# RetNet attention and snake layer on one core: a new order of steps for the first blocks, constants made on the chip

## The chip, the cores and the metric

The kernel runs on one core of a Trainium2 chip. The metric is the device time of one execution in microseconds (us), lower is better. Five engines work side by side, each through its own queue in order: TensorE (PE) multiplies, VectorE (DVE), ScalarE (ACT) and GpSimd (POOL) work on elements, SyncE (SP) issues transfers. ACT and POOL can issue transfers as well.

## The reference, cut to what matters

```python
def _attn_ref(q, k, v):              # q, k, v: 8 batches, 8 heads, 576 tokens, 64 wide, float32
    scores = scale * np.matmul(q, k.transpose(0, 1, 3, 2))
    gamma = 1.0 - 2.0 ** (-5.0 - np.arange(H))
    Dmat = np.where(rel >= 0, gamma[:, None, None] ** rel[None, :, :], 0.0)   # rel = i - j
    return np.matmul(scores * Dmat[None], v)

def _moe_ref(x, w_in, w_out, alpha):  # x: the attention's output as 4608 x 512
    h = x @ w_in                      # 512 x 2048
    s = np.sin(alpha * h)
    g = h + s * s / (alpha + 1e-09)
    return g @ w_out                  # 2048 x 512
```

## The kernel before

Eight batches of 576 tokens are cut into two tiles p of 256 tokens each and an end of 64 tokens (a 512 KB load brings one tile of q, k or v); the eight ends together make a ninth block. So there are nine blocks of 512 rows for the snake layer: block n is the first 512 tokens of batch n. A batch has four chunks c of 128 tokens, whose sums of k times v are carried from one to the next with a decay.

The steps, by the names that the code gives them:

- `load` lets SP issue one 512 KB load into one of six buffers; a load waits until the cast of the load six places before it has emptied the buffer. `load_w_in(g)` and `load_w_out(g)` let POOL issue a quarter of a weight matrix, cast to float16 on the way; group g of w_in serves the projections 4g to 4g+3.
- `cast` turns q and k to float16 with their decay factors, v without, on the engine named (V is DVE, A_ is ACT, G_ is POOL); the last argument picks a half of the tile. `turn` transposes a tile on PE with the identity (8 products), `take` copies the result out; `crossed` does both by a transposing transfer of SP instead.
- `scores(p, y, bank)` multiplies k by q (16 products), `masked` applies the mask and copies to float16 on DVE. `outer` makes the chunk sums (32 products a tile); `take_sum`, `evict` and `evict_bank` copy them out, `next_sum` (DVE) and `more` (POOL) carry the sum on, `to_state` scales it to float16. `values(p, same, bank)` multiplies scores by v in two groups, `add_states` adds the carried part, `keep` copies the result to the input x of the block.
- `project(n, u, bank)` multiplies block n by column group u of w_in (four products of 512 columns, or two times four of 256), `sine` (ACT), `square` (named engine) and `product` (DVE) make the snake function, and only the product frees the bank. `gemm2(n, u, bank)` adds a quarter of the second multiplication for row group u // 4 (part u % 4 needs `load_w_out(u % 4)`), `finish` copies out and lets SP store.
- `keep_busy(k, bank, m)` issues k products of m columns on zeros that nothing reads.

PSUM has six places: h0, h1, h2 and op of one bank, m0 and m1 of two. A step that wants a place waits until the last reader of the one before is done.

The order within each engine is the order of a list written out by hand for blocks 0 to 2 (lines 593 to 1073); waits between engines follow from the data and the places. Then a loop over n from 3 to 8 (line 1078) runs 16 units per block, each a projection of block n and a `gemm2` of block n - 1, with batch n + 1's attention between; `relay` names the engine through which PE is told that the first group of values is done. In block 3, batch 4's scores and chunk sums stand at units 0, 4 and 8; in the later blocks the scores stand at units 3 and 8 and the chunk sums were made a block earlier.

The identity (for `turn`) and the mask (for `masked`) are constants in memory that ACT's queue loads at the start, behind the decay factors `cn` and ahead of alpha and a small identity `eye` (for `turn_alpha`).

## Time and profile before

| | |
|---|---|
| median of 3 runs | 312.68 us (312.37 to 313.18) |
| profiled execution | 312.64 us |
| its span, first to last instruction | 310.9 us |
| granted TensorE clock over the span | 0.995 |
| busy: PE, DVE, ACT, POOL | 296.9, 206.9, 182.5, 140.8 us |
| moved by transfers | 49.96 MB |

Busy time of PE contains the drain of its products, so a full row does not yet mean that it runs at its peak. In rows of the order of time the columns are start and duration in us, engine, line, operation, output and inputs, shape and count; in brackets stands the idle time before the row and what ended it. A row can hold several instructions merged. In rows of groups the columns behind the bar are busy us, mean ns of one, and idle us before.

### The profile page before, as it was taken

What the parts mean: (1) busy time and instruction counts of PE and PEld (TensorE: products, weight loads), DVE (VectorE), ACT (ScalarE), POOL (GpSimd) and SP (SyncE); (2) the same over time, 40 slices, a digit from 0 to 9 for tenths busy, and PEclk for the clock granted to TensorE, in tenths of its full rate; (3) what the DMA queues carried; (4) which work ended last, traced back from release to release, by engine and by line L of the source; (5) the groups of instructions that cost most, each with busy time, mean ns of one, the idle gap of its engine ahead of it and who ended that gap; (6) DMA issues with size and microseconds to landing.
All of it is one profiled execution on the core that took longest, in us unless ns stands there. A gap on an engine that the chain in (4) does not pass through costs nothing.

```text
span 310.9 us, 7835 instructions
## 1 busy us (share of the span) xinstructions
PE 296.9 (96%) x3238; PEld 149.8 (48%) x3238; DVE 206.9 (67%) x284; ACT 182.5 (59%) x291; POOL 140.8 (45%) x151
## 2 busy tenths in 40 slices
PE   8669989999999999999999999999999999999995
PEld 3444645445554544454445444544454454444443
DVE  2578998689778798575766676656676745655600
ACT  1327952678457767775677567756764556455411
POOL 2855665984919656988275927470030000000000
PEclk9998999999999999999999999999999999999999
DMA  8999999899897679959799969863431111111133
GB/s 208 289 230 261 227 251 257 211 235 222 215 252 222 103 117 309 235 92 184 176 299 164 244 177 282 108 135 84 105 78 44 34 36 36 34 34 35 39 92 75
DMA packets 103108, 49.96 MB, mean 161 GB/s; under 512 B 44944, under 2 KB 98592, under 8 KB 103072
## 3 DMA queue, kind: packets, MB, share of 16 engines
q1 hardware_dynamic: 98192, 44.99, 65.1%
q0 software_dynamic: 4224, 4.19, 8.0%
q8 instruction: 25, 0.41, 0.6%
q10 hardware_dynamic: 656, 0.28, 0.4%
q14 instruction: 11, 0.09, 0.1%
HBM read 36.85 MB, written 9.44 MB: 149 GB/s over the span
## 4 chain that ended last, share of the span: by engine, by line
PE 83%; DMA 7%; DVE 3%; ACT 3%; issue 2%; POOL 0%; ACTq 0%; DVEq 0%
PE ops L552 38%; PE hps L509 37%; DMA w_in<-in_moe_w_in_dram 3%; PE o L374 3%; PE sc L334 3%; DMA v<-in_v_dram 2%; ACT s_t L517 2%; DMA q<-in_q_dram 1%; PE kv L275 1%; DVE q L162 1%; DVE gT L533 1%; DVE ss_t L528 1%; PE o L396 1%; ACT ss_t L526 1%; POOL v L105 0%
## 5 line engine op out<-in xcount | busy, mean ns | idle before, releaser
L552 PE MATMUL ops<-w_out,gT 128*128 128x512 f16 (+2 forms) x592 | 143.4, 374 | 1.3 <-DMA w_out<-in_moe_w_out_dram 1.2
L517 ACT ACTIVATE s_t<-hps,alpha_t 128x512 f16<-128x512 f32 x144 | 97.7, 685 | 75.0 <-PE hps L509 74.4
L533 DVE SCALAR_TENSOR_TENSOR gT<-ss_t,inva,hps 128x512 f16<-128x512 f16 x144 | 106.0, 745 | 50.9 <-ACT ss_t L526 46.6
L509 PE MATMUL hps<-xT,w_in 128*128 128x512 f16 (+1 forms) x568 | 128.5, 361 | 2.1 <-DVE gT L533 1.2
L509 PEld LDWEIGHTS <-w_in 128*128 128x128 f16 x632 | 61.3, 98 | 66.4 <-issue 3.3
L552 PEld LDWEIGHTS <-gT 128*128 128x128 f16 x592 | 56.0, 98 | 64.2 <-issue 2.0
L528 DVE TENSOR_TENSOR ss_t<-s_t 128x512 f16<-128x512 f16 x67 | 38.6, 576 | 22.0 <-ACT s_t L517 21.5
L526 ACT ACTIVATE ss_t<-s_t 128x512 f16<-128x512 f16 x69 | 43.3, 631 | 1.6 <-DVE gT L533 0.5
L345 DVE TENSOR_TENSOR ret<-sc,mask 128x1024 f16<-128x1024 f32 x32 | 38.8, 1219 | 3.8 <-PE sc L334 3.8
L162 POOL TENSOR_TENSOR k<-k,cn 128x1024 f16<-128x1024 f32 (+1 forms) x17 | 29.4, 1730 | 23.9 <-DMA k<-in_k_dram 23.9
L103 ACT COPY osb<-ops 128x512 f32<-128x512 f32 (+1 forms) x33 | 19.2, 580 | 17.2 <-PE ops L552 13.9
L162 POOL TENSOR_TENSOR q<-q,cn 128x512 f16<-128x512 f32 (+1 forms) x16 | 24.6, 1553 | 7.7 <-DMA q<-in_q_dram 7.7
L317 POOL TENSOR_TENSOR kvs<-s,kvs 128x256 f32<-128x256 f32 x23 | 17.2, 747 | 5.2 <-ACT kvs L103 3.7
L103 ACT CAST xT<-o 128x1024 f16<-128x1024 f32 (+1 forms) x14 | 13.3, 957 | 9.0 <-PE o L396 8.9
L146 POOL TENSOR_TENSOR ks<-ks,cn 128x512 f16<-128x512 f32 x4 | 4.2, 1042 | 28.0 <-PE o L374 25.3
L509 PE MATMUL hps<-xS,w_in 128*128 128x512 f16 x64 | 16.4, 379 | 0.0
L528 POOL TENSOR_TENSOR ss_t<-s_t 128x512 f16<-128x512 f16 x8 | 9.3, 1163 | 14.7 <-ACT s_t L517 14.4
L316 POOL TENSOR_TENSOR s<-kvs,cn 128x256 f32<-128x256 f32 x23 | 14.1, 613 | 3.6 <-ACT kvs L103 3.3
L105 POOL CAST v<-v 128x1024 f16<-128x1024 f32 (+1 forms) x15 | 15.1, 1005 | 0.9 <-DMA v<-in_v_dram 0.8
L309 POOL TENSOR_TENSOR s<-kvs,cn 128x256 f16<-128x256 f32 x19 | 12.1, 639 | 6.2 <-DVE kvs L105 4.2
L103 ACT COPY kvs<-kv 128x256 f32<-128x256 f32 (+2 forms) x15 | 7.9, 548 | 10.1 <-PE kv L275 8.4
L374 PE MATMUL o<-ret,v 64*64 64x128 f16 x512 | 12.1, 220 | 1.5 <-DVE ret L345 0.7
(53 smaller groups left out, 135.1 us busy)
## 6 DMA issues: line engine op xcount, KB each, us to landing
out_dram<-osb SPq DMA_DIRECT2D x70, 128.0 KB, 3.4
q<-in_q_dram SPq DMA_DIRECT2D x16, 512.0 KB, 7.2
k<-in_k_dram SPq DMA_DIRECT2D x16, 512.0 KB, 5.2
v<-in_v_dram SPq DMA_DIRECT2D x16, 512.0 KB, 6.4
w_in<-in_moe_w_in_dram POOLq DMA_DIRECT2D x4, 512.0 KB, 9.6
w_out<-in_moe_w_out_dram POOLq DMA_DIRECT2D x4, 512.0 KB, 9.6
ks<-in_k_dram SPq DMA_DIRECT2D x8, 128.0 KB, 4.7
qs<-in_q_dram SPq DMA_DIRECT2D x8, 128.0 KB, 3.7
```

The costliest lines, as they stand in the source:

```text
L103: eng.copy(d_, s_)
L105: eng.tensor_copy(d_, s_)
L162: eng.tensor_tensor(dst[:, a0:a1].rearrange("p a r t d -> p t (a r) d"), t_.rearrange("p (t a) x -> p t a x", t=2)[:, :, a0:a1].rearrange( ...
L317: nc.gpsimd.tensor_tensor(self.kvs[:, c], s32, self.kvs[:, c], ADD)
L345: nc.vector.tensor_tensor(ret.rearrange("p t (z x) -> p (t z) x", z=2), sc.rearrange("p t (z x) -> p (t z) x", z=2), mask[:, 0:256].unsque ...
L374: made.append(matmul(o[t][halves(e), c : c + 128], v16[halves(g), 4 * t + 2 * x + e, r, :], self.ret[p, x][halves(g), t, m : m + 128], sta ...
L509: matmul(hps_of[n, fc][0][:, cols], w_in16[:, a, fc * P : (fc + 1) * P], xs[n][:, a, cols], start=(a == 0 and part != 1), stop=(a == KT - ...
L517: nc.scalar.activation(s_t, hps, mybir.ActivationFunctionType.Sin, bias=0.0, scale=alpha_t[:, fc : fc + 1],)
L526: nc.scalar.activation(ss_t, s_t, mybir.ActivationFunctionType.Square)
L528: eng.tensor_tensor(ss_t, s_t, s_t, MULT)
L533: nc.vector.scalar_tensor_tensor(gT[n][:, fc, :], ss_t, inva[:, fc : fc + 1], hps, MULT, ADD)
L552: matmul(ops[n, c, cols.start][:, cols], gT[n][:, fk, c * P : (c + 1) * P], w_out16[:, fk, cols], start=(fk == 0), stop=(fk == FC - 1), sk ...
```

## The change

The list for blocks 0 to 2 is replaced. k is loaded and turned ahead of q; 12 idle products of 512 columns stand at the start and 7 of 256 columns after batch 0's last chunk sums, where 24, 4 and 1 of 512 stood before. Batch 0's casts, masks and carried sums go mostly to DVE, batch 1's second tile (`q` and `k` of p = 1) is turned before the first projection, the weight groups are loaded in the order 1, 0, 2, 3, and four projections of block 1 (one of them half done) stand ahead of the first `gemm2` of block 0. Batch 4's chunk sums, which block 3 made before, stand at the end of the list, so that block 3 runs as blocks 4 to 6 do; both relays of blocks 3 to 5 go through POOL, where one went through SP. The identity and the mask are made by POOL with `memset` and `affine_select`; their two loads are gone. `wait_for_w_out` is not called any more.

The diff, with the two lists cut to their beginnings:

```diff
-    tok = 2 * ii + hi
-    mask_np = np.concatenate(
-        [(2 * ii + r)[:, None] <= tok[None, :] for r in range(2)] + [ii[:, None] <= np.arange(64)[None, :]], axis=1
-    ).astype(np.float16)
-
-    ident_dram = nc.inline_tensor(np.eye(P, dtype=np.float16), name="rt_ident")
-    mask_dram = nc.inline_tensor(mask_np, name="rt_mask")
...
+    def make_constants():
+
+        ge = mybir.AluOpType.is_ge
+        nc.gpsimd.memset(ident, 0.0)
+        nc.gpsimd.affine_select(
+            out=ident, in_=ident, compare_op=mybir.AluOpType.not_equal, fill=1.0,
+            base=0, pattern=[[-1, P]], channel_multiplier=1,
+        )
+        nc.gpsimd.memset(mask, 1.0)
+        for g in range(2):
+            m = mask[halves(g), 0:256].rearrange("p (r g i) -> p r g i", r=2, g=2)
+            nc.gpsimd.affine_select(
+                out=m, in_=m, compare_op=ge, fill=0.0,
+                base=0, pattern=[[-1, 2], [1, 2], [2, 64]], channel_multiplier=-2,
+            )
+            m = mask[halves(g), 256:320]
+            nc.gpsimd.affine_select(
+                out=m, in_=m, compare_op=ge, fill=0.0, base=0, pattern=[[1, 64]], channel_multiplier=-1,
+            )
+
     with tc.manual_schedule():
         nc.scalar.dma_start(cn, cn_dram.ap())
-        nc.scalar.dma_start(ident, ident_dram.ap())
-        nc.scalar.dma_start(mask, mask_dram.ap())
+        make_constants()
...
-keep_busy(2, "h0")
-keep_busy(8, "op")
-keep_busy(10, "op")
-keep_busy(4, "op")
-load(0, "q", 0)
-cast(0, "q", 0, G_, (1,))
-cast(0, "q", 0, V, (0,))
-turn(0, "q", 0, "h0")
-load(0, "k", 0)
-cast(0, "k", 0, G_, (0,))
-cast(0, "k", 0, V, (1,))
-turn(0, "k", 0, "op")
-take(0, "q", 0, A_)
-take(0, "k", 0, V, (0,))
-take(0, "k", 0, V, (1,))
-load(0, "k", 1)
-cast(0, "k", 1, G_)
-load(0, "q", 1)
-cast(0, "q", 1, V)
-load_w_in(0)
-turn(0, "k", 1, "h1")
-take(0, "k", 1, A_)
-at[0].scores(0, 1, "m0")
-keep_busy(4, "h2")
-load(0, "v", 0)
-at[0].masked(0, 1)
-turn(0, "q", 1, "h2")
-take(0, "q", 1, V)
-cast(0, "v", 0, G_)
-at[0].outer((0,), "op", "h0")
-load_w_in(1)
-at[0].take_sum(0, A_)
-load(0, "v", 1)
-cast(0, "v", 1, G_)
-at[0].scores(1, 0, "m1")
-at[0].outer((1,), "op", "h1")
-at[0].masked(1, 0)
-at[0].take_sum(1, A_)
-at[0].more(1)
-at[0].scores(0, 0, "m0")
-at[0].masked(0, 0)
-at[0].scores(1, 1, "m1")
-at[0].masked(1, 1)
-keep_busy(1, "h2")
-at[0].values(0, False, "m0")
-turn_alpha()
-at[0].to_state(0, G_)
-at[0].to_state(1, V)
-at[0].take_sum(2, A_)
-at[0].more(2)
-at[0].next_sum(3)
-at[0].to_state(2, G_)
-load_w_in(2)
-load(1, "q", 0)
-at[0].values(0, True)
-at[0].add_states(0)
-at[0].keep(0, A_)
-at[0].values(1, False, "h2", "h0")
-at[0].values(1, True)
-at[0].add_states(1)
-project(0, 0, "m1", 0)
-load(1, "k", 0)
-at[0].keep(1, A_, V)
-project(0, 0, "m1", 1)
-take_alpha()
-sine(0, 0)
-cast(1, "q", 0, V, (1,))
-cast(1, "q", 0, V, (0,))
-square(0, 0, V)
...
+keep_busy(1, "op")
+keep_busy(6, "h0")
+load(0, "k", 0)
+cast(0, "k", 0, V)
+keep_busy(5, "op")
+load(0, "q", 0)
+load(0, "k", 1)
+load(0, "q", 1)
+turn_alpha()
+cast(0, "q", 0, V)
+cast(0, "k", 1, V)
+cast(0, "q", 1, G_, (1,))
+turn(0, "q", 0, "h0")
+turn(0, "k", 0, "h1")
+turn(0, "k", 1, "h2")
+take(0, "k", 0, A_)
+take_alpha()
+take(0, "q", 0, V)
+at[0].scores(0, 1, "m0")
+cast(0, "q", 1, V, (0,))
+take(0, "k", 1, V)
+at[0].scores(0, 0, "m1")
+at[0].masked(0, 0)
+load(0, "v", 0)
+cast(0, "v", 0, A_)
+load_w_in(1)
+turn(0, "q", 1, "op")
+load(0, "v", 1)
+take(0, "q", 1, A_)
+at[0].outer((0,), "h0", "h1")
+at[0].masked(0, 1)
+at[0].scores(1, 1, "m0")
+load_w_in(0)
+at[0].take_sum(0, A_)
+at[0].scores(1, 0, "m1")
+cast(0, "v", 1, V, (0,))
+cast(0, "v", 1, V, (1,))
+at[0].outer((1,), "op", "h2")
+load_w_in(2)
+at[0].to_state(0, G_)
+load(1, "k", 1)
+cast(1, "k", 1, G_)
+keep_busy(7, "h0", 256)
+turn(1, "k", 1, "h0")
+take(1, "k", 1, A_)
+at[0].next_sum(1)
+at[0].next_sum(2)
+at[0].to_state(1, V)
+at[0].masked(1, 1)
+at[0].values(0, False, "m0")
+at[0].masked(1, 0)
+at[0].values(0, True)
+at[0].add_states(0)
+at[0].keep(0, A_)
+at[0].to_state(2, V)
+at[0].values(1, False, "m1")
+at[0].values(1, True)
+at[0].add_states(1)
+load_w_in(3)
+at[0].keep(1, A_)
+load(1, "q", 1)
+cast(1, "q", 1, V, (0,))
+cast(1, "q", 1, G_, (1,))
+turn(1, "q", 1, "h1")
+take(1, "q", 1, A_)
+load(1, "k", 0)
+project(0, 5, "h0", 0)
+project(0, 5, "h0", 1)
+project(0, 4, "op", 0)
+project(0, 4, "op", 1)
+sine(0, 5)
+sine(0, 4)
+square(0, 4, A_)
+project(0, 6, "h2")
+sine(0, 6)
+square(0, 6, G_)
+project(0, 2, "h1")
+at[1].scores(1, 1, "m0")
+sine(0, 2)
+invert_alpha()
+square(0, 2, A_)
+project(0, 0, "h0")
+sine(0, 0)
+project(0, 3, "m1")
+sine(0, 3)
+at[0].next_sum(3)
+at[0].to_state(3, V)
+cast(1, "k", 0, G_)
+square(0, 5, V)
+product(0, 5)
+product(0, 4)
+at[1].masked(1, 1)
+project(0, 9, "m0")
+sine(0, 9)
+product(0, 6)
+product(0, 2)
+square(0, 0, G_)
+square(0, 3, V)
+load_w_out(0)
+square(0, 9, A_)
+project(0, 7, "op", 0)
+project(0, 7, "op", 1)
+sine(0, 7)
+project(0, 1, "h2")
+sine(0, 1)
+product(0, 3)
+load(1, "q", 0)
+product(0, 9)
+cast(1, "q", 0, G_)
+product(0, 0)
+square(0, 7, A_)
+load(1, "v", 0)
+product(0, 7)
+square(0, 1, A_)
+at[1].scores(1, 0, "m1")
+turn(1, "k", 0, "h1")
+take(1, "k", 0, V)
+project(0, 15, "m0")
+product(0, 1)
+sine(0, 15)
+square(0, 15, A_)
+product(0, 15)
+at[1].masked(1, 0)
+cast(1, "v", 0, G_)
+project(0, 8, "op")
+sine(0, 8)
+square(0, 8, G_)
+turn(1, "q", 0, "h0")
+project(0, 13, "h1")
+load(1, "v", 1)
+product(0, 8)
+cast(1, "v", 1, G_)
+take(1, "q", 0, A_)
+sine(0, 13)
+at[1].outer((0,), "h2", "h0")
+at[1].take_sum(1, A_)
+load_w_out(1)
+at[1].take_sum(0, A_)
+at[1].to_state(0, G_)
+at[1].more(1)
+load_w_out(2)
+at[1].scores(0, 1, "m1")
+square(0, 13, A_)
+at[1].scores(0, 0, "m0")
+at[1].masked(0, 0)
+at[1].outer((1,), "op", "h2")
+product(0, 13)
+at[1].take_sum(3, A_)
+at[1].masked(0, 1)
+project(0, 10, "h0")
+project(0, 12, "h2")
+project(0, 11, "h1")
+at[1].to_state(1, G_)
+sine(0, 10)
+at[1].values(1, False, "m0")
+at[1].values(0, False, "m1")
+at[1].values(0, True)
+at[1].add_states(0)
+at[1].next_sum(2)
+at[1].values(1, True)
+at[1].to_state(2, V)
+at[1].keep(0, V)
+at[1].add_states(1)
+square(0, 10, V)
+sine(0, 11)
+product(0, 10)
+sine(0, 12)
+project(0, 14, "op")
+square(0, 11, G_)
+project(1, 0, "m1", 0)
+at[1].keep(1, A_)
+square(0, 12, A_)
+load_w_out(3)
+product(0, 12)
+sine(0, 14)
+square(0, 14, A_)
+project(1, 7, "m0")
+sine(1, 7)
+product(0, 11)
+project(1, 1, "h0")
+product(0, 14)
+square(1, 7, A_)
+product(1, 7)
+load(2, "q", 1)
+project(1, 8, "h2")
+gemm2(0, 0, "h1")
+project(1, 0, "m1", 1)
+project(1, 9, "op")
+sine(1, 8)
+gemm2(0, 1, "h1")
...
+at[4].outer((0, 1), "m1")
...
-        h, m = cycle(("h2", "h0", "h1")), cycle(("m0", "m1"))
+
+        h, m = cycle(("h1", "h2", "h0")), cycle(("m0", "m1"))
-        S_ = nc.sync
-                if n == 3:
-                    at_unit(0, lambda: A.scores(0, 0, next(m)), lambda: A.scores(0, 1, next(m)))
-                    behind(0, lambda: A.masked(0, 0))
-                    behind(1, lambda: A.masked(0, 1))
-                    at_unit(4, lambda: A.outer((0, 1), next(m)), lambda: A.scores(1, 0, next(m)), lambda: A.evict((0, 1)))
-                    behind(4, lambda: A.chain((0, 1, 2, 3)), lambda: A.masked(1, 0))
-                    at_unit(8, lambda: A.scores(1, 1, next(m)))
-                    behind(8, lambda: A.masked(1, 1))
-                else:
-                    at_unit(3, lambda: A.scores(0, 0, next(m)), lambda: A.scores(0, 1, next(m)))
-                    behind(3, lambda: A.masked(0, 0))
-                    behind(4, lambda: A.masked(0, 1))
-                    at_unit(8, lambda: A.scores(1, 0, next(m)), lambda: A.scores(1, 1, next(m)))
-                    behind(8, lambda: A.masked(1, 0))
-                    behind(9, lambda: A.masked(1, 1))
-                at_unit(12, lambda: A.values(0, False, next(m), relay=G_), lambda: A.values(1, False, next(m), relay=S_ if n < 6 else G_))
+                at_unit(3, lambda: A.scores(0, 0, next(m)), lambda: A.scores(0, 1, next(m)))
+                behind(3, lambda: A.masked(0, 0))
+                behind(4, lambda: A.masked(0, 1))
+                at_unit(8, lambda: A.scores(1, 0, next(m)), lambda: A.scores(1, 1, next(m)))
+                behind(8, lambda: A.masked(1, 0))
+                behind(9, lambda: A.masked(1, 1))
+                at_unit(12, lambda: A.values(0, False, next(m), relay=G_), lambda: A.values(1, False, next(m), relay=G_))
```

More of the change, by code (lines that the diff above doesn't have):

```diff
@@ L915 @@
         product(1, 13)
[L916 to L930 removed]
+        finish(0, 2)
         at[2].values(0, True)
@@ new lines @@
+        at[2].to_state(3, V)
+        product(1, 11)
+        gemm2(1, 2, "op")
+        project(2, 5, "h2", 0)
+        project(2, 5, "h2", 1)
+        at[3].outer((0, 1), "m0")
+        at[3].scores(0, 1, "m1")
+        square(2, 1, G_)
+        product(2, 1)
+        at[3].evict((0, 1), A_)
+        sine(2, 5)
+        at[3].masked(0, 1)
+        at[3].more(1)
+        square(2, 5, A_)
+        product(2, 5)
+        load(4, "v", 0)
+        load(4, "v", 1)
+        at[3].more(2)
+        cast(3, "q", 1, G_, (0,))
```

595 lines of the change are left out of this document (230 added, 365 removed).

## The prediction

> **What bounds the kernel now.** I read the page first, for the shares and the clock.
>
> ```profile
> span 310.9 us, 7835 instructions
> PE 296.9 (96%) x3238; PEld 149.8 (48%) x3238; DVE 206.9 (67%) x284; ACT 182.5 (59%) x291; POOL 140.8 (45%) x151
> PE 83%; DMA 7%; DVE 3%; ACT 3%; issue 2%; POOL 0%; ACTq 0%; DVEq 0%
> ```
>
> TensorE (PE) is the bound, and the chain that ended last is mostly its own work. Next came the table of busy time by stretch; each row gives PE, PEld, DVE, ACT and POOL busy, then the granted clock, the DMA share and GB/s.
>
> ```profile
> 15.00:20.00 5.00, 2.30 (x98) 1.68 (x98) 4.68 (x8) 0.37 (x1) 4.76 (x8) 1.00 1.20 220
> 20.00:25.00 5.00, 3.74 (x67) 2.17 (x67) 2.77 (x5) 2.29 (x4) 1.05 (x2) 0.72 1.18 258
> 25.00:30.00 5.00, 5.00 (x27) 2.55 (x26) 4.73 (x9) 3.79 (x6) 2.39 (x4) 0.94 1.17 267
> 35.00:40.00 5.00, 5.00 (x43) 3.55 (x41) 4.56 (x8) 4.62 (x10) 2.82 (x3) 1.00 1.18 235
> 145.00:155.00 10.00, 10.00 (x77) 4.61 (x75) 7.26 (x10) 5.87 (x10) 3.85 (x4) 1.00 0.93 139
> ```
>
> In the loop (last row) PE never pauses. The loss lies at the start: PE is busy for less than half of 15 to 20 us, then runs at a granted clock of 0.72. From 25 us on it is full, but DVE and ACT are nearly full beside it, and the transfer engines are full throughout. So I listed PE's order of time, to find each place where it waits.
>
> ```profile
> 1.22 7.69 PE L565 MATMUL idle<-zero 128*128 128x512 f16 x24 [1.22 <-DVE zero L591]
> 21.77 1.53 PE L509 MATMUL hps<-xT,w_in 128*128 128x256 f16 x8 [0.15 <-ACT xT L103]
> 23.96 9.62 PE L509 MATMUL hps<-xT,w_in 128*128 128x512 f16 x48 [0.66 <-DMA w_in<-in_moe_w_in_dram]
> 33.41 0.61 PE L195 MATMUL tr<-ident,k 128*128 128x128 f16 x8
> 33.86 1.03 PE L509 MATMUL hps<-xT,w_in 128*128 128x512 f16 x4
> 42.39 1.02 PE L552 MATMUL ops<-w_out,gT 128*128 128x512 f16 x4 [1.19 <-DMA w_out<-in_moe_w_out_dram]
> 66.66 1.03 PE L509 MATMUL hps<-xT,w_in 128*128 128x256 f16 x8 [0.69 <-DVE gT L533]
> 109.99 1.89 PE L509 MATMUL hps<-xT,w_in 128*128 128x512 f16 x8 [0.55 <-DVE gT L533]
> 119.39 0.71 PE L275 MATMUL kv<-v,k 64*64 64x64 f16 x64
> ```
>
> The first projection starts at 21.77 us. Behind it PE waits four times: 0.66 (w_in), 1.19 (w_out), 0.69 and 0.55 us (a bank that a product still held). A row contains the drain of its last matmul: the turn at 33.41 shows 0.61, yet the next work starts 0.45 later. So a wait costs about 0.16 more than its idle time, and the four together 3.09 + 4 x 0.16 = 3.7 us.
>
> The profiled execution took 312.64 us: the span of 310.9 and 1.74 around it. The median of the runs is 312.68. I sum against 312.64. The tail and the loop blocks 4 to 7 keep their work; the 64 products of batch 4's chunk sums (0.71 us at 119.39) move from block 3 into the list, at no net cost. What the change is worth is therefore the change in PE's lost time before block 3.
>
> **Part 1: the way to the first projection.** The new list hands nearly all of batch 0 to DVE, so I add up DVE's program order. It needs the landings and these durations:
>
> ```profile
> 5.08 0.69 DVE L162 TENSOR_TENSOR q<-q,cn 128x512 f16<-128x512 f32 x1 [3.91 <-DMA q<-in_q_dram]
> 7.16 0.69 DVE L162 TENSOR_TENSOR k<-k,cn 128x512 f16<-128x512 f32 x1 [1.39 <-DMA k<-in_k_dram]
> 9.05 1.90 POOL L162 TENSOR_TENSOR k<-k,cn 128x1024 f16<-128x1024 f32 x1 [0.30 <-DMA k<-in_k_dram]
> 10.82 1.22 DVE L162 TENSOR_TENSOR q<-q,cn 128x1024 f16<-128x1024 f32 x1 [0.22 <-DMA q<-in_q_dram]
> 12.68 1.03 POOL L105 CAST v<-v 128x1024 f16<-128x1024 f32 x1 [0.85 <-DMA v<-in_v_dram]
> 13.65 0.69 DVE L105 COPY qT<-tr 128x1024 f16<-128x1024 f16 x1 [0.39 <-PE tr L195]
> 12.03 1.23 DVE L345 TENSOR_TENSOR ret<-sc,mask 128x1024 f16<-128x1024 f32 x1
> 18.56 0.56 DVE L309 TENSOR_TENSOR s<-kvs,cn 128x256 f16<-128x256 f32 x1
> 19.05 0.84 DVE L304 SCALAR_TENSOR_TENSOR kvs<-kvs,cn,kv 128x64 f32<-128x64 f32 x4
> 48.16 0.46 DVE L105 CAST v<-v 128x512 f16<-128x512 f32 x1
> 20.46 0.93 PE L374 MATMUL o<-ret,v 64*64 64x128 f16 x32
> 5.12 1.55 POOL L162 TENSOR_TENSOR q<-q,cn 128x512 f16<-128x512 f32 x1 [4.67 <-DMA q<-in_q_dram]
> ```
>
> The six loads of batch 0 land 1.85 us apart (5.0, 7.1, 9.0, 10.8, 12.65, so 14.5), whichever tile is first. DVE: cast of k0 5.1 + 1.22 = 6.3; of q0 7.15 + 1.22 = 8.4; of k1 10.25; take of q0 and half a cast of q1 to 11.6; take of k1 to 12.3; two masks to 14.8; the two halves of v1 to 15.7; two next_sums to 17.4; to_state to 17.95; two masks to 20.4; to_state(2) to 20.95; half a cast of the new q(1,1) to 21.65. PE's steps stand inside these times. Behind the last mask PE has two groups of values (0.93 by its row, drain included) and the states, and then the turn of q(1,1), 0.45 behind its cast. The first projection starts at about 22.2, 0.4 later than now. But two turns of batch 1 (2 x 0.45) are done by then that came later before: net -0.5. The 12 idle products, at 0.32 each on the mean of the 24 in the first row and 0.43 at half speed (twice 0.86 / 4, below), end by 6.4, in a gap; the 7 short ones lie in the wait for k(1,1)'s cast on POOL, about 16 to 18: 0. Cover gone, each would cost its 0.1 us.
>
> POOL makes identity and masks with two memsets and five selections, which the trace does not show. The nearest rows:
>
> ```profile
> 0.24 0.10 POOL L1184 MEMSET const-float32-0.0<- 128x1 f32 x1 [0.24 <-issue]
> 29.56 1.03 POOL L528 TENSOR_TENSOR ss_t<-s_t 128x512 f16<-128x512 f16 x1 [2.61 <-ACT s_t L517]
> ```
>
> Seven at 0.10 to 1.03 us are 0.7 to 7.2 us, ended by 7.6. The identity, made first, is wanted at 8.4, POOL's half cast at 10.8. I take 0. Two small transfers fewer ahead of the loads can only gain a little, down to -0.3.
>
> **Part 2: the clock.** Five us at 0.72 and five at 0.94 withhold 5 x 0.28 + 5 x 0.06 = 1.7 us; about 0.5 of it fell into the wait for w_in, where it cost nothing. PE is again sparse from 6 to 22, so I expect one such stretch again, now under continuous projections: +0.5. The ends are -1.2 (no slow stretch) and +2.2 (two).
> The Trainium skill, "TensorE: Matmul & The Clock Gate", section "Why this matters for your kernels", warns of idle gaps beyond about 3 us and gives back the full clock after about 3.4 us of work. This speaks against taking 17 idle products out. The trace agrees in so far as the slow stretch followed the sparse one.
>
> **Part 3: waits that go.** Projections (0,5), (0,4), (0,6) now use w_in's group 1, loaded first; the first multiplication by w_out comes after 19 projections, not 15, so both DMA waits go. The two waits for DVE (0.69, 0.55) belong to the old order. All four: -3.7. What is late next is part 4.
>
> **Part 4: waits that come.** Block 0's elementwise work is squeezed in with batch 1's masks.
>
> ```profile
> L517 ACT ACTIVATE s_t<-hps,alpha_t 128x512 f16<-128x512 f32 x144 | 97.7, 685 | 75.0 <-PE hps L509 74.4
> L526 ACT ACTIVATE ss_t<-s_t 128x512 f16<-128x512 f16 x69 | 43.3, 631 | 1.6 <-DVE gT L533 0.5
> L533 DVE SCALAR_TENSOR_TENSOR gT<-ss_t,inva,hps 128x512 f16<-128x512 f16 x144 | 106.0, 745 | 50.9 <-ACT ss_t L526 46.6
> 40.57 1.00 ACT L103 COPY qT<-tr 128x1024 f16<-128x1024 f16 x1
> 16.07 0.37 ACT L103 COPY kvs<-kv 128x256 f32<-128x256 f32 x1 [1.17 <-PE kv L275]
> 26.54 0.42 DVE L528 TENSOR_TENSOR ss_t<-s_t 128x512 f16<-128x512 f16 x1
> 14.39 0.42 PE L334 MATMUL sc<-qT,kT 64*64 64x128 f16 x16 [0.19 <-DVE qT L105]
> ```
>
> PE from 22.2: two projections at half speed (2 x 1.72), eight at 0.86, the 1.03 of a row less its drain (6, 2, 0, 3, 9, 7, 1, 15), two score groups (0.35 each behind one another) and a turn reach 33.7. Projection (0,8) then needs the bank that product (0,7) frees. DVE has queued from about 28.1 one mask, one square (0.4) and six products (4.5), and product 7 also waits for ACT's square: ready near 34.8. Wait 1.0. Then (0,8), a turn and (0,13) reach 37.0, where outer wants the bank that ACT's take of q(1,0) empties. ACT has from 24.0 eleven sines (7.5), six squares (3.8) and the take (1.0), 36.3 without a gap, 37.4 with the gaps at its start: wait 0 to 0.8, I take 0.7. A chunk sum on ACT holds the next bank 0.4 more. Together 2.1. With the ordering so tight the bounds are 0 and 4.5, which doubles each wait. DVE's queue from 29.3 to the end of block 0 (fourteen products 10.4, three masks 3.7, two squares, a take, a sum, a state and a keep 4.1) is 18.2 us, done at 47.5 to 49; PE's, with these waits, near 50. So nothing more piles up.
>
> From 50 to 110 us I found cushions of 1 to 4 us at the steps of batches 2 and 3. Banks wanted 0.1 to 0.2 us early occur a few times: I take 0.5, bounds 0 and 2. Loop: both relays now sit in POOL's queue; the second stands right behind the first, the casts after both: 0.
>
> **Sum:** -0.5 + 0.5 - 3.7 + 2.1 + 0.5 = -1.1; 312.64 - 1.1 = 311.5, against the median 312.68 a gain of 0.4%.
>
> **The rivals.**
>
> *The late tile (slower).* The first projection now stands behind q(1,1), the eighth load, and POOL's w_in transfers share the engines.
>
> ```profile
> 10.89 0.93 POOL L93 DMA_DIRECT2D w_in<-in_moe_w_in_dram  x1
> 24.30 1.14 POOL L162 TENSOR_TENSOR k<-k,cn 128x512 f16<-128x512 f32 x1 [3.95 <-DMA k<-in_k_dram]
> ```
>
> The eighth load landed at 24.3 where 1.85 spacing gives 18.2, because w_in, issued at 10.89, crowded it from about 16.3 on: 8 us for a load of 1.85, 4.3 times slower. The first w_in is now issued behind POOL's half cast (1.14 to 1.55 from 10.8), at 12 to 12.4, some 1.2 to 1.5 us later; the load then lacks 0.35 to 0.65 of its 1.85 when the crowding begins and lands at 19.2 to 20.5. It decides from 20.95 on: each us later costs one. Landing at 24.3 as now, half a cast on POOL (1.1) and the turn put the first projection at 26: +3.8, 315.3. For it: the margin is only 0.5 to 1.7 us. Against: the later issue.
>
> *The elementwise engines (slower).* If part 4 meets its upper bounds, +2.4 and +1.5: up to 315.4; half of it gives 313.5 to 314. For it: 4.56 and 4.62 of 5 us busy at 35 to 40.
>
> *Two slow stretches (same).* The stretch lost 1.7 us of clock in this execution; a second one under continuous projections is +1.7: 313.2. For it: PE stays sparse longer, without its fillers; against: projections leave no gap from 22.2 on. The Trainium skill's same page, section "What's actually happening", has windows that run free of the kernel's start, so that a boundary can fall badly; no row here shows two in a row.
>
> *No new waits (faster).* Part 4 at nothing: -3.7, 308.9.
>
> **How the numbers follow.** A measurement of this kernel tells 0.3%, 0.94 us, from no change. Forecast 0.42; late tile 0.17; elementwise engines 0.18; two stretches 0.10; no new waits 0.13. Faster: 0.13 and four fifths of the forecast, 0.46. Slower: both slow cases and a little of the third, 0.37. The rest, 0.17, within. The forecast's own range is 310.5 to 312.5; the range over the cases is 308.8 to 315.5.
>
> **What would show it.** Right: first projection near 22.2, no wait of PE on w_in or w_out, one stretch below full clock between 20 and 30, waits of about 2 us on ACT and DVE between 33 and 40, block 3 starting a little sooner for the work done. Wrong: a PE wait for q(1,1)'s cast or turn, POOL busy with the constants beyond 8 us, or waits behind 50 us that sum to over 2.

## The result, and the profile after

The changed kernel is slower: 314.64 us median (20 runs, 312.91 to 317.72) against 312.61 (20 runs of the kernel before, 312.03 to 314.59), a ratio of 1.0056 with an interval of 1.0034 to 1.0078. Here and below, a ratio leaves out the executions in the slower state (317.72 here), so it need not be the quotient of the medians. The forecast was 311.5, a gain; the median lies inside the range over all cases, on the other side of no change, and outside the forecast's own 310.5 to 312.5. The executions of the changed kernel fall into two groups, nine of the 20 at 312.9 to 313.3 us and eleven at 314.3 to 317.7, so a profile of each is read here: one of 313.06 us (span 311.3) and, from a second set of runs of the same kernel, one of 317.0 (span 315.3). The clock averaged over the span doesn't tell the groups apart (0.976 to 0.989 in the short executions, 0.975 to 0.995 in the long ones), so one profile of the long group can't say what each of its executions pays.

The page of the 313.06 us profile, the shares and the chain that ended last:

```profile
span 311.3 us, 7778 instructions
PE 297.3 (95%) x3212; PEld 150.7 (48%) x3212; DVE 211.3 (68%) x297; ACT 184.4 (59%) x291; POOL 132.4 (43%) x143
PE 75%; DMA 10%; DVE 7%; SPq 2%; ACT 2%; POOL 1%; issue 1%; DVEq 0%; ACTq 0%; POOLq 0%
```

Work moved from POOL (140.8 to 132.4) to DVE (206.9 to 211.3), and DVE's share of the chain rose from 3% to 7%. PE's order of time in the same profile shows where that is; the brackets give PE's idle time and what ended it:

```profile
22.48 0.88 PE L189 MATMUL tr<-ident,q 128*128 128x128 f16 x8
23.20 3.66 PE L503 MATMUL hps<-xT,w_in 128*128 128x256 f16 x24
...
38.17 0.45 PE L269 MATMUL kv<-v,k 64*64 64x64 f16 x32 [0.26 <-POOL v L99]
...
43.62 0.31 PE L390 MATMUL o<-qT,s 64*64 64x128 f16 x8 [0.78 <-DVE s L303]
...
60.63 0.71 PE L269 MATMUL kv<-v,k 64*64 64x64 f16 x64 [0.16 <-DVE gT L527]
...
96.74 0.42 PE L328 MATMUL sc<-qT,kT 64*64 64x128 f16 x16 [1.29 <-DVE gT L527]
...
108.55 2.75 PE L503 MATMUL hps<-xT,w_in 128*128 128x512 f16 x12
112.88 1.02 PE L546 MATMUL ops<-w_out,gT 128*128 128x512 f16 x4 [1.58 <-DVE gT L527]
```

The first projection starts at 23.20. The waits for w_in and w_out are gone. Two long new waits, 1.29 and 1.58 us, both for a place that DVE's product frees, lie at 96.74 and 112.88. The second of them is in the loop: of the three projections in the row at 108.55, the third, from 110.28 on, is the first of block 3. The same view of the 317.0 us profile:

```profile
21.62 0.62 PE L189 MATMUL tr<-ident,q 128*128 128x128 f16 x8
22.08 2.19 PE L503 MATMUL hps<-xT,w_in 128*128 128x256 f16 x16
...
40.32 0.45 PE L269 MATMUL kv<-v,k 64*64 64x64 f16 x32 [2.44 <-POOL v L99]
...
64.53 0.70 PE L269 MATMUL kv<-v,k 64*64 64x64 f16 x64 [1.59 <-DVE gT L527]
...
100.65 0.42 PE L328 MATMUL sc<-qT,kT 64*64 64x128 f16 x16 [1.28 <-DVE gT L527]
...
116.79 1.02 PE L546 MATMUL ops<-w_out,gT 128*128 128x512 f16 x4 [1.58 <-DVE gT L527]
```

Here the first projection starts 1.1 us **earlier**, yet the execution ends 3.9 later: outer((1,)) of batch 1 waits 2.44 in place of 0.26, outer of batch 2 waits 1.59 in place of 0.16. The two late waits of the other profile are in this one too, with the same length. PE also waits twice for w_in, 0.35 at 25.48 and 0.40 at 29.10. What differs ahead of 22 us is the clock (columns as before: PE, PEld, DVE, ACT, POOL busy, granted clock, DMA share, GB/s), first in the 313.06 us profile, then in the 317.0 one:

```profile
5.00:10.00 5.00, 2.62 (x21) 1.33 (x19) 3.72 (x4) 0.68 (x1) 0.00 (x0) 0.94 1.17 290
10.00:15.00 5.00, 4.06 (x96) 3.42 (x100) 4.66 (x7) 2.63 (x5) 4.14 (x5) 0.50 1.17 290
15.00:20.00 5.00, 4.57 (x91) 3.20 (x79) 5.00 (x12) 0.96 (x1) 4.04 (x4) 0.50 1.20 243
20.00:25.00 5.00, 4.82 (x100) 4.19 (x98) 2.83 (x10) 3.46 (x5) 0.00 (x0) 0.69 1.20 218
```

```profile
5.00:10.00 5.00, 2.60 (x21) 1.86 (x18) 3.69 (x4) 0.00 (x0) 0.00 (x0) 0.80 1.17 289
10.00:15.00 5.00, 3.33 (x115) 2.68 (x115) 4.74 (x7) 3.32 (x5) 4.12 (x5) 0.85 1.17 290
15.00:20.00 5.00, 2.62 (x83) 1.89 (x75) 5.00 (x12) 1.01 (x1) 4.00 (x4) 1.00 1.20 243
20.00:25.00 5.00, 4.73 (x100) 3.37 (x100) 3.47 (x12) 4.16 (x5) 0.00 (x0) 1.00 1.19 216
```

In the faster execution the clock is at half from 9.4 to 23.06 us, in the slower one only from 8.05 to 11.46. So the full clock made this execution no faster, and the question is what an earlier first projection sets off. POOL's queue tells, first in the 313.06 us profile, then in the 317.0 one:

```profile
31.19 0.80 POOL L90 DMA_DIRECT2D w_out<-in_moe_w_out_dram  x1
33.26 1.89 POOL L156 TENSOR_TENSOR q<-q,cn 128x1024 f16<-128x1024 f32 x1 [1.26 <-DMA q<-in_q_dram]
...
37.09 1.03 POOL L99 CAST v<-v 128x1024 f16<-128x1024 f32 x1
```

```profile
30.15 0.81 POOL L90 DMA_DIRECT2D w_out<-in_moe_w_out_dram  x1
33.21 1.89 POOL L156 TENSOR_TENSOR q<-q,cn 128x1024 f16<-128x1024 f32 x1 [2.26 <-DMA q<-in_q_dram]
...
39.23 1.04 POOL L99 CAST v<-v 128x1024 f16<-128x1024 f32 x1 [2.14 <-DMA v<-in_v_dram]
```

load_w_out(0) stands behind POOL's square(0,0). With earlier projections POOL reaches it at 30.15 in place of 31.19. The transfer engines were full already; the load of v(1,1), in SP's queue, then lands at 39.17 in place of 36.78, 2.4 us later for an issue 1.0 earlier. POOL's cast and PE's outer((1,)) wait for it. The same two times, read from all thirteen traces of the changed list and of the edits of it that follow, show a step and not a slope: in the four with the issue between 27.32 and 30.49, v(1,1) landed at 39.17 to 39.50; in the nine with it between 31.19 and 36.53, at 36.76 to 36.97. Three of the nine start the first projection as early as the 317.0 us profile does (21.98 to 22.32). Why the load falls on one side or the other is open.

### The profile page after: what moved, and what is told of

Same layout as the page of the kernel before. It is cut to its first block, busy times and chain, and to the rows that moved or that the text cites. A ratio compares the mean times of both kernels' runs of the same rounds, so it can differ in the third digit from the quotient of the medians.

```text
span 311.3 us, 7778 instructions
## 1 busy us (share of the span) xinstructions
PE 297.3 (95%) x3212; PEld 150.7 (48%) x3212; DVE 211.3 (68%) x297; ACT 184.4 (59%) x291; POOL 132.4 (43%) x143
## 4 chain that ended last, share of the span: by engine, by line
PE 75%; DMA 10%; DVE 7%; SPq 2%; ACT 2%; POOL 1%; issue 1%; DVEq 0%; ACTq 0%; POOLq 0%
PE ops L546 37%; PE hps L503 32%; DMA q<-in_q_dram 8%; DMA v<-in_v_dram 2%; PE sc L328 2%; PE o L368 2%; DVE v L99 2%; DVE gT L527 2%; PE kv L269 1%; SPq L108 1%; DVE ss_t L522 1%; DVE s L303 1%; POOL v L99 1%; PE o L390 1%; POOL q L156 1%
## 5 line engine op out<-in xcount | busy, mean ns | idle before, releaser
L503 PEld LDWEIGHTS <-w_in 128*128 128x128 f16 x616 | 59.3, 98 | 64.4 <-issue 0.9
L156 POOL TENSOR_TENSOR k<-k,cn 128x1024 f16<-128x1024 f32 (+1 forms) x16 | 26.3, 1655 | 25.3 <-DMA k<-in_k_dram 25.3
L97 ACT COPY osb<-ops 128x512 f32<-128x512 f32 (+1 forms) x36 | 20.9, 580 | 20.8 <-PE ops L546 19.4
L156 POOL TENSOR_TENSOR q<-q,cn 128x1024 f16<-128x1024 f32 (+1 forms) x14 | 24.7, 1771 | 14.0 <-DMA q<-in_q_dram 13.7
L311 POOL TENSOR_TENSOR kvs<-s,kvs 128x256 f32<-128x256 f32 x20 | 15.1, 755 | 2.2 <-ACT kvs L97 0.6
L310 POOL TENSOR_TENSOR s<-kvs,cn 128x256 f32<-128x256 f32 x20 | 12.2, 611 | 8.9 <-ACT kvs L97 8.6
L303 POOL TENSOR_TENSOR s<-kvs,cn 128x256 f16<-128x256 f32 x19 | 13.2, 696 | 1.3 <-ACT kvs L97 0.6
L328 PE MATMUL sc<-qT,kT 64*64 64x128 f16 x512 | 11.7, 231 | 1.8 <-DVE gT L527 1.3
L328 PEld LDWEIGHTS <-kT 64*64 64x64 f16 x512 | 8.8, 113 | 7.6 <-issue 6.5
L522 POOL TENSOR_TENSOR ss_t<-s_t 128x512 f16<-128x512 f16 x7 | 7.6, 1089 | 11.3 <-ACT s_t L511 8.1
```

What stands on the lines that cost most here:

```text
L97: eng.copy(d_, s_)
L156: eng.tensor_tensor(dst[:, a0:a1].rearrange("p a r t d -> p t (a r) d"), t_.rearrange("p (t a) x -> p t a x", t=2)[:, :, a0:a1].rearrange( ...
L303: (eng or nc.gpsimd).tensor_tensor(self.state_of(c), self.kvs[:, c], g1.unsqueeze(2).to_broadcast([P, 4, D]), MULT)
L328: matmul(sc[halves(g), t, c : c + 128], kT[halves(t), 2 * a + r, halves(g)], qT[halves(t), 2 * a : 2 * a + 2, halves(g)], start=(z == 0 an ...
L503: matmul(hps_of[n, fc][0][:, cols], w_in16[:, a, fc * P : (fc + 1) * P], xs[n][:, a, cols], start=(a == 0 and part != 1), stop=(a == KT - ...
L522: eng.tensor_tensor(ss_t, s_t, s_t, MULT)
```

## The experiments

The theory after the result had two parts. **A1:** load_w_out(0) crowds the load of v(1,1), by an amount set by the moment of its issue. **A2:** behind 50 us DVE frees three places late, since its work runs beside POOL's casts and is stretched. Rivals: the constants made by POOL, the clock itself, or engines so full that any wait removed returns elsewhere. Each ratio is to runs of the kernel before taken beside the experiment (medians 312.50 to 312.92).

**The changed kernel again**, without an edit.

> The changed kernel once more, unaltered, for a second profile and more times. Its 20 executions fell in two groups, ten at 312.9 to 313.3 us and ten at 314.3 to 317.7, and the one profiled was of the low group (313.06). Theory of the clock: the products on the way to the first projection are so sparse that the granted clock falls to half somewhere between 6 and 27 us, at a moment that differs from execution to execution; where the half clock lasts beyond the first projection the execution falls in the high group. It expects the two groups again, and if the profile is of the high group, half clock behind 23 us and nothing else that moved. Rival, the late tile: in the high group the second tile of batch 1's q lands after 21 us and the first projection starts at 24 or later, with the clock as it was.

Median 316.97 over ten runs (313.06 to 318.88), ratio 1.0097 (1.0058 to 1.0137) to the kernel before; it gave the 317.0 us profile above. Two groups came again, but neither theory of them holds: in this long execution the clock was full from 11.46 on, and q(1,1) had landed at 17.72.

**More idle products**, to keep the clock up:

```diff
-        keep_busy(5, "op")
+        keep_busy(12, "op")
...
         at[0].scores(0, 0, "m1")
+        keep_busy(4, "h0")
...
+        keep_busy(3, "h1")
         take(1, "k", 1, A_)
```

> The changed kernel with 14 more idle products of 512 columns: 7 more at the start, 4 behind the first scores, 3 behind the turn of batch 1's k; all in gaps of PE. Theory of the clock: the full clock is kept until about 19 or 22 us, the first projection starts at 22.2 to 22.6 instead of 23.2, the high group vanishes or shrinks to executions within 1.7 us of the low one, median 312 to 313. Late tile as the cause of the high group: two groups as before, median 314 to 315.

Median 319.46 (317.31 to 320.26, 4 runs), ratio 1.019 (1.0139 to 1.024). The clock did stay full until 40 us, and fell under the projections instead:

```profile
20.00:25.00 5.00, 4.88 (x100) 3.29 (x95) 3.47 (x12) 4.33 (x6) 0.00 (x0) 1.00 1.20 217
40.00:45.00 5.00, 4.62 (x44) 1.94 (x43) 2.77 (x7) 1.06 (x2) 4.36 (x7) 0.66 0.96 227
```

The first projection stood at 22.08 and the wait for v at 2.29, as in the 317.0 us profile. So a clock held up to the first projection doesn't make this list faster. Ahead of 23 us it mostly covers waits for DVE, which in both profiles above is busy for all of 15 to 20 us. Most of the 2.45 us by which this execution (319.45) is longer than the 317.0 us one is a wait of 1.76 at 205.52 for DVE's product, which neither profile of the changed kernel has; what brings it there is open.

**The constants loaded again**, as the kernel before did:

```diff
-        make_constants()
+        nc.scalar.dma_start(ident, ident_dram.ap())
+        nc.scalar.dma_start(mask, mask_dram.ap())
```

> The changed kernel with identity and mask loaded through ACT's queue as before the change. In the trace of the changed kernel POOL is done with them at 3.0 us and the identity is wanted at 8.2, so the theory is that they cost and bring nothing: same as the changed kernel within 0.3 us in the low group, the loads of batch 0 landing up to 0.2 us later. Rival: the two small transfers less had moved the loads earlier by 0.2 to 0.3 us, and the second tile of q with them; then this one is slower by 0.3 to 1 us, and the high group is larger.

Median 316.13 (313.4 to 318.2, ten runs), ratio 1.0084 (1.0046 to 1.0122), with the same waits (2.39 for v, 1.6 for outer of batch 2, 1.3 and 1.6 at the late two). The constants are not the cause. What making them on the chip brings is small: with them loaded, q(1,1) landed at 18.07 in place of 17.72 and the first projection started at 22.42 in place of 22.08, in two profiles with nearly the same stretch of half clock (8.20 to 11.61 and 8.05 to 11.46).

**Batch 4's v casts on ACT, its q load earlier:**

```diff
-        cast(4, "v", 0, V)
+        cast(4, "v", 0, A_)
...
-        cast(4, "v", 1, V)
+        cast(4, "v", 1, A_)
...
         crossed(3, 1, "q")
+        load(4, "q", 0)
...
-        load(4, "q", 0)
         cast(4, "q", 0, V, (1,))
```

> The changed kernel with batch 4's two casts of v on ACT instead of DVE, and the load of batch 4's first q tile issued behind the second transposing transfer of batch 3's q instead of behind batch 3's keep. Theory of the late waits: PE's waits of 1.29 us at 96.7 and 1.58 us at 112.9, both for a product on DVE, come from DVE being held by those casts (2.39 and 1.73 us beside POOL's casts) and by a wait for that load; both vanish, the low group moves from 313.1 to 310 to 311, the high group by as much. Rival: DVE is late there by its own queue of products and squares, ACT gets late instead, and less than 1 us is won.

Median 314.5 (311.86 to 316.37, ten runs), ratio 1.0052 (1.0013 to 1.0091). The wait at scores (96.74 in the 313.06 us profile) went; the one at the loop's start stayed at 1.46, so q(4,0)'s load was not its cause. PE waits there for product(2,14), which stood in DVE's queue behind the two casts of q(4,0) (2.25 us), a state, half a keep and a square of 2.09 us. Outer of batch 2 waited 1.6 in this profile, though v(1,1) had landed at 36.76, so the longer wait there doesn't need the crowded load.

**load_w_out(0) later.** It moves behind POOL's cast(1,v,0):

```diff
-        load_w_out(0)
         square(0, 9, A_)
...
         cast(1, "v", 0, G_)
+        load_w_out(0)
```

> The changed kernel with one line moved: load_w_out(0) stands behind POOL's cast(1,v,0) in place of square(0,3), so it is issued at about 36.1 us in place of 30.1 to 31.2. Theory A (w_out(0) crowds SP's load of v(1,1), and how much depends on when POOL gets to issue it): v(1,1) lands at 35 to 37 us whatever the clock did before, POOL's cast of it starts at about 37, PE's wait for POOL's v at outer((1,)) is under 0.5 us in place of 2.44, w_out is still in time for gemm2(0,0) (no wait), and the median comes down by 2 to 3 us from 316 to 317, to 313.5 to 314.5. Rival B (the longer executions come from something else that goes with an early full clock, the crowded load only accompanies it): v(1,1) lands early, but the median stays at 315.5 or more. Rival C (w_out is then late): PE waits over 1 us for w_out between 46 and 51 us.

Median 314.83 (314.19 to 316.33, 6 runs), ratio 1.008 (1.006 to 1.0101). v(1,1) landed at 36.76 and w_out was in time, as A1 has it, though the clock was full from 19 us on. But PE still waited 1.13 for POOL's v: the issue takes 0.81 of POOL's queue, ahead of the cast. The cause of the landing is met, the price was moved rather than removed, and the median is above the 313.5 to 314.5 expected.

**load_w_out(0) earlier**, ahead of cast(1,k,0):

> The opposite dose: load_w_out(0) stands ahead of POOL's cast(1,k,0), so it is issued about 3 us earlier than in the changed kernel, at 27.3 to 28.3 us. Theory A: v(1,1) lands at 39.5 to 41.5 us in every execution, PE waits 2.5 to 4.5 us for POOL's v at outer((1,)), and the median is 316.5 to 319. Rival B: no change of the median, 314.5 to 317.

Median 317.25 (317.23 to 319.86, all four runs above 317), ratio 1.017 (1.0141 to 1.0199). The issue came at 27.32, 2.8 us sooner than in the 317.0 us profile. The wait for v did not grow (1.31 + 1.09 = 2.40 against 2.44) but spread over both chunk sums of batch 1, and 0.71 for q(1,0) came on top:

```profile
35.89 0.62 PE L189 MATMUL tr<-ident,q 128*128 128x128 f16 x8 [0.71 <-POOL q L156]
...
38.69 0.45 PE L269 MATMUL kv<-v,k 64*64 64x64 f16 x32 [1.31 <-POOL v L99]
...
40.67 0.45 PE L269 MATMUL kv<-v,k 64*64 64x64 f16 x32 [1.09 <-POOL v L99]
```

None of the four executions is short, which is what A1 expects; four are few, since eleven of the 30 runs of the unedited kernel were short (up to 313.4). v(1,1) landed at 39.35, a little before the 39.5 to 41.5 expected; v(1,0) and q(1,0) bore part of the delay.

**The three late places:**

```diff
         sine(1, 15)
...
+        square(1, 15, A_)
         project(1, 10, "op")
...
-        square(1, 15, V)
...
+        product(1, 15)
         square(1, 3, V)
...
         square(1, 10, V)
-        product(1, 15)
...
-        cast(4, "v", 0, V)
+        cast(4, "v", 0, A_)
...
-        cast(4, "v", 1, V)
+        cast(4, "v", 1, A_)
...
-        sine(2, 13)
         sine(2, 14)
-        square(2, 14, V)
+        square(2, 14, A_)
+        product(2, 14)
+        sine(2, 13)
...
         product(2, 13)
-        product(2, 14)
```

> The changed kernel with three waits of PE for banks behind 50 us taken away by other orders on ACT and DVE: square(1,15) on ACT and product(1,15) ahead of square(1,3) (outer of batch 2, wait 0.33 to 1.79 us at 60 to 64); cast(4,v,0) and cast(4,v,1) on ACT (wait 1.45 at 96.7); sine(2,14) ahead of sine(2,13), square(2,14) on ACT, product(2,14) right behind it (wait 1.74 at 112.9). Theory A (DVE, stretched beside POOL's casts, frees these three banks late): all three waits fall below 0.4 us, and the median falls by 3 to 4.5 us against the changed kernel, to 311.5 to 313.5 (the crowded load of v(1,1) stays). Rival B (the elementwise engines are full there, so a wait removed comes back at the next bank): under 1.5 us gained, and a new wait of over 1 us between 60 and 120 us.

Median 313.61 (309.64 to 315.56, ten runs), ratio 0.9984 (0.9949 to 1.0019). The median is a little above the 311.5 to 313.5 expected. The profiled execution took 309.71, 3.35 less than the 313.06 of the changed kernel; both reach the first projection late, behind stretches of half clock (23.08 and 23.20), and both have v(1,1) in time. Two more executions took 309.64 and 309.68, where the short group of the changed kernel stood at 312.9 to 313.3. The view of PE's waits from 22 to 120 us holds nothing but this:

```profile
PE o L390 <- DVE s L303: 0.8, 1, 0.8
PE kv L269 <- POOL v L99: 0.3, 1, 0.3
PE hps L503 <- DVE gT L527: 0.2, 1, 0.2
```

All three waits are gone and none came back in this profile, against the rival of full engines. That DVE frees the three places late, and what that costs, is shown. That stretched work is why it is late rests on the durations of its rows (in the last section): the edit changes the order and takes work off DVE, and no run has DVE's order as it was with POOL out of the way. The longer executions remain (seven of ten at 311.64 to 315.56), as they should with load_w_out(0) left where it was.

**Both** (load_w_out(0) behind cast(1,v,0), and the three places):

> Both together: load_w_out(0) behind cast(1,v,0), and the three orders for the banks. Theory A: the two gains add up, since they lie at different places: 309 to 310.5 us, under the kernel before by 0.6 to 1.1%, with PE's lost time before the loop down from 24 to 20 to 21 us. Rival B: they do not add, 312 or more.

Median 312.46 (310.93 to 314.37, 12 runs), ratio 0.999 (0.9971 to 1.0008): less than the sum, and inside rival B's 312 or more. The profiled execution of 310.93 has one wait over 0.8 left, 1.07 for POOL's v, the price that the issue has in POOL's queue.

**Both, and square(0,8) from POOL to DVE** to shorten that queue:

> As the run with both edits together, and square(0,8) goes from POOL to DVE. In that run PE still waited 1.07 us for POOL's v at outer((1,)), though v(1,1) had landed at 36.9: the w_out(0) issue (0.81) and square(0,8) (1.05) stood ahead of the cast in POOL's queue. Theory A (POOL's queue is what is late there): the cast starts at 36.9 to 37.1, the wait falls below 0.4, DVE makes the square while it waited for POOL's anyway, and the median comes to 310.5 to 312, the best execution to 309 to 310. Rival B: DVE has no room (its mask and product(0,8) move back), a wait of 0.5 us or more comes at the banks behind it, and the median stays at 312 to 313.

Median 312.25 (310.42 to 314.01), ratio 0.9976 (0.9951 to 1.0). The cast came at 37.02 as expected, but the square on DVE took 1.18 us beside it, product(0,8) came later, and PE waited as long for that:

```profile
37.14 1.18 DVE L522 TENSOR_TENSOR ss_t<-s_t 128x512 f16<-128x512 f16 x1
38.36 0.75 DVE L527 SCALAR_TENSOR_TENSOR gT<-ss_t,inva,hps 128x512 f16<-128x512 f16 x1
```

```profile
39.16 0.44 PE L269 MATMUL kv<-v,k 64*64 64x64 f16 x32 [1.24 <-DVE gT L527]
57.05 1.02 PE L546 MATMUL ops<-w_out,gT 128*128 128x512 f16 x4 [0.83 <-DMA w_out<-in_moe_w_out_dram]
```

The first view is DVE's, the second PE's. Rival B has this step. The later w_out groups now were late as well: moving the issue back has its own end. Two further waits came, 0.59 at 76.11 for a transposing transfer of k and 1.05 at 84.73 for DVE's product, so here removed waits did return elsewhere.

**The same with the 14 idle products:**

> The same with 14 more idle products of TensorE while it waits for batch 0 (7 more at the start, 4 behind scores(0,0), 3 ahead of take(1,k,1)). With the waits of this list gone, does a clock that stays up help? Theory A (the clock's stretch at half speed before 23 us lies over waits for DVE, so it costs under 1 us, and the idle products stand in the way when they overlap work): 0 to 2 us slower than the same list without them. Rival B (the clock is what is left; an unbroken clock is worth 1 us or more): 1 to 2 us faster.

Median 315.88 (314.19 to 318.88, 6 runs), ratio 1.0107 (1.0065 to 1.0148), 3.6 us above the list without them, more than the 0 to 2 expected. The clock was full to the end of the list and beyond (0.998 over the span). PE waited 1.3 for w_in (0.94 at once, at 26.05), 1.9 at 46.9 for nothing that the profile shows, and 1.93 at 200.7 for a product. The gain of 1 us or more that rival B wants from an unbroken clock is not there once the products that keep it up are paid for. What the clock alone is worth this run doesn't tell, and where all of the 3.6 comes from stays open.

**A wait for the moment of the issue.** load_w_out(0) keeps its place, in a gap in which POOL waits for q(1,0) anyway, but is held until ACT has made sine(0,7):

```diff
-        load_w_out(0)
         square(0, 9, A_)
...
         sine(0, 7)
+        told(sines[0, 7], G_)
+        load_w_out(0)
```

> The changed kernel with one wait on POOL: load_w_out(0) stands where it stood (behind square(0,3), ahead of cast(1,q,0)), but is issued only when ACT has made sine(0,7), at about 32.1 us. POOL waits there for q(1,0) until 33.1 anyway, so its casts are not pushed back, unlike in the run with the issue behind cast(1,v,0). Theory A (the moment of this issue alone decides the crowding of v(1,1)): v(1,1) lands by 37.0, PE waits under 0.5 us for it in every execution, also where the clock is full early; no w_out wait; the executions above 315.5 go, and the median is 313 to 314.5 (the three bank waits stay). Rival B (an early clock costs the time elsewhere): median 315.5 to 317 as before.

Median 313.84 (313.04 to 315.82, 12 runs), ratio 1.004 (1.0017 to 1.0063): none above 316, where six of the ten repeated runs of the changed kernel lay above 316.9. Two of the twelve, 315.67 and 315.82, are still above the 315.5 that theory A allows. The profile shows the issue held, and no wait for v(1,1) behind it:

```profile
32.22 0.80 POOL L90 DMA_DIRECT2D w_out<-in_moe_w_out_dram  x1 [1.01 <-ACT s_t L511]
33.05 1.91 POOL L156 TENSOR_TENSOR q<-q,cn 128x1024 f16<-128x1024 f32 x1
35.40 1.04 POOL L99 CAST v<-v 128x1024 f16<-128x1024 f32 x1 [0.43 <-DMA v<-in_v_dram]
36.39 1.04 POOL L522 TENSOR_TENSOR ss_t<-s_t 128x512 f16<-128x512 f16 x1
37.38 1.04 POOL L99 CAST v<-v 128x1024 f16<-128x1024 f32 x1
```

PE's wait was 0.75, not under 0.5: behind the 0.43 that v(1,0) came late, POOL's cast of v(1,1) started 0.29 later than in the 313.06 us profile. The interval of the ratio still overlaps those of both sets of runs of the changed kernel, so A1 rests on the landings in the profiles more than on this median.

**That wait and the three places together:**

> That wait on POOL together with the three orders for the banks behind 50 us. Theory A (the two causes add): best execution 309 to 309.8, median 309.5 to 311, under the kernel before by 0.5 to 1%. Rival B (each removed wait returns at another bank, as in the run with square(0,8) on DVE): median 312 or more.

Median 311.4 (310.08 to 311.78, 7 runs), ratio 0.9957 (0.9938 to 0.9976): faster than both kernels, with a narrow spread. Against the run with the wait alone (313.84) the three orders brought 2.4 us, where they brought 3.35 in the short execution above. Neither the median nor the best execution reached what theory A gives (309.5 to 311, 309 to 309.8), and rival B's 312 was not reached either: the gains add in the main, and one wait came back. It is PE's wait for the second half of batch 3's keep on DVE, at 110.58, now the longest (1.23):

```profile
PE hps L503 <- DVE xT L99: 1.2, 1, 1.2
PE o L390 <- DVE s L303: 0.8, 1, 0.8
PE kv L269 <- POOL v L99: 0.3, 1, 0.3
```

## Why the prediction failed, by its own steps

- **First projection, forecast 22.2.** Right with the clock up (22.08), 1.0 short with the clock at half (23.20), since the values and the turn ahead of it took longer (the turn 0.88 against 0.62). DVE's chain came as added up, within 0.5 at each step. The late-tile rival did not happen: q(1,1) landed at 17.7.
- **The constants, forecast 0.** Right. POOL had made them by 3.0 us. The gain of up to 0.3 that the prediction allowed for two transfers fewer is about what the run with loaded constants shows (0.35).
- **The clock, forecast +0.5.** The stretch came, but ahead of the projections and longer; the clock was back at 23.06. Before, 1.2 us of it lay under projections, so this term by itself is -1.2, the end of its range; what the half clock cost stands in the first projection, 1.0 late. The two terms together are 0.5 - 1.2 = -0.7, where the forecast has -0.5 + 0.5. No step asked what an earlier first projection sets off further on.
- **Waits that go, -3.7.** Right in the 313.06 us profile. In the 317.0 one w_in came back at 0.7 (0.35 + 0.40 of idle time).
- **Waits that come in block 0, +2.1.** 0.20, 0.26 and 0.78 of idle time in the 313.06 us profile, 1.7 with the drain of 0.16 for each: near in size. Only the first, for a product, is where it was looked for; the others are for POOL's cast of v and for DVE's state. In the 317.0 us profile 2.2 more for v(1,1). I had priced the crowding of a load by POOL's transfers for w_in and q(1,1) alone, and not asked the same of load_w_out(0) and v(1,1), where it happened.
- **Waits for DVE behind 50 us, +0.5 up to 110 us and 0 for the loop. This is the step that failed.** Three waits for DVE's products cost 0.33 + 1.45 + 1.74 = 3.5 us from one product of PE to the next in the 313.06 us profile, and 1.76 + 1.45 + 1.74 = 5.0 in the 317.0 one. By the prediction's own division the first two belong to 50 to 110 us: 1.8, inside its bounds of 0 and 2, in the 313.06 us profile, and 3.2, past them, in the 317.0 one. The third stands at 112.88, behind block 3's first projection. The prediction counted PE's lost time ahead of block 3 only, looked at the relays alone in the loop, and put 0. Its own sign of being wrong, waits behind 50 us that sum to over 2, came. It shows no working for the cushions of 1 to 4 us that it found there. The rows that it gives for DVE's square and half cast of v, 0.42 and 0.46, are short ones: over the trace, the squares beside POOL's work took 0.80 on the mean, and half casts of k and v up to 0.87 in this profile and 1.48 in the other. Taking the three waits away gave 3.35 back.

With the measured terms the sum is -0.7 - 3.7 + 1.7 + 3.5 = +0.8, and the profiled execution stands at +0.42 to the one before. Up to block 3 the forecast was nearly met, partly by luck: block 3 starts at 110.28 in place of 110.85, with batch 4's chunk sums (0.59 from 119.39 to the next row's start in the kernel before) already done, a gain of 1.16 against the forecast's 1.1. But the terms behind it were off by -1.7 (clock), +1.0 (first projection), -0.4 (block 0) and +1.3 (50 to 110 us). The wait of 1.74 just behind turned the gain into a loss.

The rival of the elementwise engines came nearest. It priced the waits of block 0 and of 50 to 110 us at 4.5 + 2 at the upper end; in the 313.06 us profile they came to 1.7 + 1.8, and the loop's 1.74, which it did not have, to 5.2 in all. The long execution that was traced pays the crowded load and the longer wait at batch 2 on top. What the other long ones pay, no trace shows.

## What to carry to other kernels

Where one engine's operations take longer beside another engine's work, lay its queue out with the durations that they have there, not with the shortest ones. Follow the waits past the point where the two lists meet again: here the one that decided stood just behind it. A weight transfer in another queue can delay a load that is next in line by more than it was issued early (here 2.4 us for 1.0), so its place in the order is a moment in time that a faster start moves; if it must not come sooner, let it wait for something. And keeping an engine at full clock ahead of a stretch in which it waits for others gained nothing here.

## What the runs showed of the hardware

**DVE beside POOL.** DVE's orders of time in the 313.06 and the 317.0 us profile, the three squares ahead of product(1,15):

```profile
57.90 1.92 DVE L522 TENSOR_TENSOR ss_t<-s_t 128x512 f16<-128x512 f16 x3
59.74 1.39 DVE L527 SCALAR_TENSOR_TENSOR gT<-ss_t,inva,hps 128x512 f16<-128x512 f16 x2
```

```profile
60.94 2.79 DVE L522 TENSOR_TENSOR ss_t<-s_t 128x512 f16<-128x512 f16 x3
```

Three squares at 0.42 would be 1.26; a POOL cast of 1.93 from 60.85 lies beside those of the second. Ahead of the other two waits, at 96.74 and 112.88, stand these rows of the 313.06 us profile:

```profile
91.33 2.39 DVE L99 CAST v<-v 128x1024 f16<-128x1024 f32 x1
...
94.30 1.73 DVE L99 CAST v<-v 128x1024 f16<-128x1024 f32 x1
...
109.99 1.52 DVE L522 TENSOR_TENSOR ss_t<-s_t 128x512 f16<-128x512 f16 x1
```

The casts lie beside two POOL casts of k (4.39 from 91.09), the square beside one of q (2.08 from 109.15). Half a tile of v took 0.41 to 0.46 in its shortest rows, so at most 0.92 for a whole one. Taken over the whole trace of the 313.06 us profile, instruction by instruction, 36 of DVE's 68 squares had no POOL work beside them and took 0.41 to 0.43; 28 had POOL at work for more than half of their time and took 0.80 on the mean, from 0.41 to 1.68, so not every overlap stretches. The 144 products took 0.73 to 0.75 in both cases. The trace of the kernel before says the same (39 squares at 0.42, 25 at 0.82 on the mean), so this could have been read ahead of the forecast. By these figures the stretch is longer than each wait: 1.92 - 1.26 = 0.66 against 0.33 at 60.63, 4.12 - 1.84 = 2.3 against 1.45 at 96.74; ahead of 112.88 it is 1.1 for the square, 0.6 for the two half casts of q(4,0) (2.00 against 2 x 0.68) and 0.4 for a state (0.83 against 0.42), together 2.1 against 1.74. The Trainium skill, "SBUF — State Buffer", section "Who interferes with whom", says that a DVE instruction with two inputs in SBUF, the on-chip memory of the tiles, contends with a GpSimd instruction that reads SBUF, as copies and casts can in DVE's two-port modes. The traces agree: the square has both inputs there, while the product, which reads one from PSUM, is not stretched.

**The clock.** The stretches at half clock last 3.41 us or a whole multiple of it: 22.18 to 25.59 before (3.41), 8.05 to 11.46 (3.41) and 9.4 to 23.06 (13.65, four times) after, 14.1 to 24.34 (10.24, three times) in the run with batch 4's v casts on ACT. The Trainium skill, "TensorE: Matmul & The Clock Gate", section "What's actually happening", has the clock decided over free-running windows of about 3.4 us, which agrees. The advice against idle gaps in the Trainium skill, "TensorE: Matmul & The Clock Gate", section "Why this matters for your kernels", is what the two runs with 14 more idle products followed: in the first the stretch at half clock moved to 40.39 to 43.80, in the second there was none, and both were slower than the list without them.
